# Running count's first copy on ScalarE, the mask on SP's queue, warm-up matmuls behind a pass's scores

## The chip, the core and the metric

The kernel runs on one core of a Trainium2 chip. A core has five engines that run side by side: TensorE (PE; its weight loads are shown apart as PEld), VectorE (DVE), ScalarE (ACT), GpSimd (POOL) and SyncE (SP), which here only issues DMAs. DMAs issued by SP, ACT and POOL go to queues of 16 DMA engines. The metric is the time of one execution in microseconds (us), as the median of several runs.

## The reference, cut to what matters

An attention with two branches feeds a mixture of experts in which each token goes to one expert (top 1).

```python
# q, k, v: 8 batches x 8 heads x 576 positions x 64
q_d = q.reshape(B, H, Sd, 4, D).mean(axis=3)          # k_d, v_d alike
out_d = sm_attn(q_d, k_d, v_d)                        # softmax attention on 144 positions
out_up = np.repeat(out_d, 4, axis=2)
mask = np.abs(pos[:, None] - pos[None, :]) < 4        # local branch: a band of 7 keys
out_local = softmax(where(mask, scale * q @ k.T, -1e9)) @ v
x = (out_up + out_local).transpose(0, 2, 1, 3).reshape(4608, 512)

logits = x @ w_gate                                   # 8 experts
e = argmax(logits); gate = softmax(logits)[e]
y = gate * (relu(x @ w1[e]) @ w2[e])                  # w1[e]: 512x1024, w2[e]: 1024x512
```

## The kernel before

**Attention in passes.** Two heads make one step, so there are 32 steps. They run as a software pipeline written out by hand: the table `PASS` lists pairs `(f, lag)`, and pass i calls `f(i - lag)` for each row of the table in order. That order is the order of the instructions on every engine. Pass i does, among others, in this order: exponentials of the local scores of step i-1 (`exp_loc`, ACT), half the transposes of the pooled branch of step i-3 (`t_d0`, PE), the row maximum of the pooled scores of step i-1 (`max_d`, DVE), the reciprocals `inv` and `inv_d` of step i-2 (DVE), the local scores of step i (`s_loc`, PE: 4 matmuls that put the band's mask into PSUM tile `pS`, line 245, and 20 with the queries and keys, line 251), `pv_loc` and `pv_d` of step i-3 (PE), `norm` (DVE), `max_loc` and `sub_loc` of step i (DVE), `t_loc` of step i-2 (PE), the pooled scores of step i (`s_d`, PE, tile `pD`), `sums` (DVE), `add_up` of step i-3 (DVE, writes `XT`) and the other half of the transposes, `t_d1`. `pS` and `pD` have one buffer each: `s_loc` waits until DVE has read the step before (`sub_loc`), `s_d` until ACT has (`exp_d`).

**Loads.** SP's queue takes, in each pass, queries and keys `qk` of step i+2 (583 KB, 3 buffers), pooled values `vd` of step i+1 (288 KB, 2 buffers; SP waits here for POOL's `vdt`, line 230), a piece of padding or of a weight (`ld_x`), and local values `vw` of step i-1 (320 KB, 2 buffers; SP waits here for `pv_loc`, line 357). POOL adds up the pooled queries, keys and values (`qkt`, `qkd`, `vdt`, `vds`). ACT's queue issues three constants at the start: `cb` (identity and a triangle), `mask` (128x640 of 2 bytes, 160 KB) and `cf` (128x276 of 4 bytes, 138 KB).

**Routing.** Every fourth pass a block of token tiles is ready: gate logits, top expert, and its row in the expert's list. The running count `crun`, 8 numbers in each partition, starts as a copy from the constants `cf` (line 925, after pass 2, on DVE); it is first read some passes later, and POOL adds to it (line 482). POOL then scatters the rows to `xs` (line 550).

**Experts.** After the passes and a tail come, for each of 8 experts, the two layers (lines 674 to 676 and 688 to 690), nearly all of it on PE.

**Warm-up matmuls.** `WARM = (9, 5, 8, 5)`: 9 matmuls of 128x512 on zeros (`wsrc`) before the first pass, then 5, 8 and 5 at the ends of passes 0, 1 and 2. Their results are not used.

```python
    for i in range(NP):
        steps(i)
        if i + 1 < len(WARM):
            warm(WARM[i + 1], i >= 3)
        if i == 2:
            nc.vector.tensor_copy(crun, cf[:, C_CAP:C_CAP + E])
```

Of the kernel before, what the change touches and what calls it, by code (L numbers as in the profile page):

```python
# [11 lines left out]
F32 = mybir.dt.float32  # L12
# [14 lines left out]
NC = NG // 2  # L27
# [15 lines left out]
NEG = -8.0e9  # L43
WARM = (9, 5, 8, 5)

# [45 lines left out]
def attention_moe_kernel(ctx: ExitStack, tc: tile.TileContext, qk, vw, vd, wg, w1, w2, cst, csb, out):  # L91
# [32 lines left out]
    maskb = p1.tile([128, B_END - B_MASK], BF, name="mask", bufs=1)  # L124
    nc.scalar.dma_start(maskb, csb[:, B_MASK:])
    load_qk(1)
# [7 lines left out]

    def warm(n, late=False):
        p = bank() if late else wp
        for _ in range(n):
            nc.tensor.matmul(p, wsrc[:, :128], wsrc, start=True, stop=True)

# [256 lines left out]
    def r_mm(m, tiles):  # L396
        c = tiles[0] * 128
        p = RS[m, "p"] = bank()
        for k, a in [(k, a) for k in (0, 2, 1, 3) for a in range(2)]:
            r = a * 64 + k // 2 * 32  # L400
            nc.tensor.matmul(p[r:r + 32, :256], wgt[:, k, :],
                             XT[m][:, k, c:c + 512].rearrange("p (u a t) -> p a u t", u=2, a=2)[:, a],
                             start=(k % 2 == 0), stop=(k % 2 == 1), tile_position=(0, r), skip_group_check=True)
        for k in range(4) if len(tiles) > 4 else ():
            r = k * 32
            nc.tensor.matmul(p[r:r + 32, 256:384], wgt[:, k, :], XT[m][:, k, c + 512:c + 640],
                             start=True, stop=True, tile_position=(0, r), skip_group_check=True)

    def r_lg(m, tiles):
        lg = RS[m, "lg"] = rp.tile([128, 384], F32, name="over", bufs=1)  # L410
        w = 256 if len(tiles) == 4 else 384
        nc.scalar.activation(lg[:, :w], RS[m, "p"][:, :w], AF.Copy)

    def r_turn(m, tiles):
        lg = RS[m, "lg"]
        p = RS[m, "p"] = bank()
        for u in range(2):
            nc.tensor.matmul(p[:, u * 64:u * 64 + 64], lg[:, u * 128:u * 128 + 128], cf[:, C_PAIR:C_PAIR + 64],
                             start=True, stop=True)
        if len(tiles) > 4:  # L420
            nc.tensor.matmul(p[:, 128:160], lg[:, 256:], cf[:, C_SUM:C_SUM + 32], start=True, stop=True)

    def r_max(m, tiles):
        T = len(tiles)
        RS[m, "pl"] = RS[m, "p"][:, :T * 32].rearrange("p (t e) -> p t e", e=32)[:, :, :E]
        RS[m, "m"] = rp.tile([128, 5], F32, name="rm")
        nc.vector.tensor_reduce(RS[m, "m"][:, :T], RS[m, "pl"], axis=AX.X, op=OP.max)

    def r_sub(m, tiles):
        T = len(tiles)  # L430
        d = RS[m, "d"] = RS[m, "p"][:, 256:296].rearrange("p (t e) -> p t e", e=E)
        nc.vector.tensor_sub(d[:, :T], RS[m, "pl"], RS[m, "m"][:, :T, None].to_broadcast([128, T, E]))

    def r_exp(m, tiles):
        T = len(tiles)
        ex = RS[m, "ex"] = rp.tile([128, 5, E], F32, name="re")
        nc.scalar.activation(ex[:, :T], RS[m, "d"][:, :T], AF.Exp)

    def r_top(m, tiles):
        T = len(tiles)  # L440
        sc = RS[m, "sc"] = RS[m, "p"][:, 320:360].rearrange("p (t e) -> p t e", e=E)
        nc.vector.scalar_tensor_tensor(sc[:, :T], RS[m, "d"][:, :T], 0.0,
                                       cf[:, None, C_DESC:C_DESC + E].to_broadcast([128, T, E]),
                                       op0=OP.is_ge, op1=OP.mult)

    def r_first(m, tiles):
        T = len(tiles)
        nc.vector.tensor_reduce(RS[m, "m"][:, :T], RS[m, "sc"][:, :T], axis=AX.X, op=OP.max)

    def r_hot(m, tiles):  # L450
        T = len(tiles)
        oh = RS[m, "oh"] = rp.tile([128, 5, E], BF, name="oh")
        nc.vector.tensor_tensor(oh[:, :T], RS[m, "sc"][:, :T], RS[m, "m"][:, :T, None].to_broadcast([128, T, E]),
                                op=OP.is_equal)

    def r_gate(m, tiles):
        T = len(tiles)
        gt = RS[m, "gt"] = rp.tile([128, 5], F32, name="gt")
        nc.vector.tensor_reduce(gt[:, :T], RS[m, "ex"][:, :T], axis=AX.X, op=OP.add)

    def r_eps(m, tiles):
        T = len(tiles)
        gt = RS[m, "gt"]
        nc.scalar.activation(gt[:, :T], gt[:, :T], AF.Copy, bias=1e-9)

    def r_place(m, tiles):
        T = len(tiles)
        oh = RS[m, "oh"]
        p = RS[m, "p"] = bank()
        nc.tensor.matmul(p[:, :T * E], trib, oh[:, :T], start=True, stop=False, skip_group_check=True)  # L470
# [30 lines left out]
    def r_last(m, tiles):
# [153 lines left out]

    def split_w2(e, f):
        if (e, f) == (0, 0):
            home("tgi", 2)
            home("ttix", 1)
            home("gap", 16)  # L660
        hi, lo = W2[e, f] = tuple(mp[f // 6].tile([128, DM], F32R, name=f"w2{n}{f}") for n in "hl")
        src = raws[place[2, e, f // 2]][:, (f % 2) * 512:(f % 2) * 512 + 512]
        nc.scalar.activation(hi, src, AF.Copy)  # L663
        nc.vector.tensor_sub(lo, src, hi)  # L664

    def s1(e, f, r=slice(0, FIRST)):
        if e not in HT:
            HT[e] = tuple(mp[0].tile([128, 8, FIRST], F32R, name=f"h{w}") for w in "hl")
        xh, xl = XH[e, 0]
        p = h_bank()[:, :r.stop - r.start]  # L670
        fs = slice(f * 128, (f + 1) * 128)
        for k in range(4):
            wh, wl = W1[e, k]
            nc.tensor.matmul(p, wh[:, fs], xh[:, k, r], start=(k == 0), stop=False)  # L674
            nc.tensor.matmul(p, wh[:, fs], xl[:, k, r], start=False, stop=False)  # L675
            nc.tensor.matmul(p, wl[:, fs], xh[:, k, r], start=False, stop=(k == 3))  # L676
# [216 lines left out]
    def ld_x(i):  # L893
# [180 lines left out]
```

## Time and profile before

| | us |
|---|---|
| median of 3 runs | 649.36 |
| lowest, highest | 646.58, 651.08 |
| profiled execution, its own time | 644.67 |
| span of the core in it, first to last instruction | 642.9 |

The profiled execution is one more run; its span and its own time are 1.8 us apart, which is launch and end. Sums below are made on the trace and so against 644.67. The passes take from 4.7 us to about 175 us of the span, a tail of routing and the first expert's loads to about 245, the experts the rest.

### The profile page before, as it was taken

Reading aid. Unit: us, or ns where it says so; the run is one execution under the profiler, and the core shown is the slowest. Engines: PE = TensorE matmul, PEld = TensorE weight load, DVE = VectorE, ACT = ScalarE, POOL = GpSimd, SP = SyncE. Lnnn points to the kernel's source line nnn. Section 1 sums busy time; section 2 is a strip of 40 time slices with the busy share of each in tenths; the row PEclk is TensorE's granted clock in tenths of the full one; section 3 lists DMA queues with packets and bytes.
Section 4 is the critical chain, followed back from the end, with each engine's and each line's share of the span. In section 5 each row is a group of like instructions: output and inputs, shape, how many; then the busy total and the mean of one; then the engine's idle time right before and its main releaser. Section 6 shows DMA issues by size and latency. Waiting matters only on the chain.

```text
span 642.9 us, 15721 instructions
## 1 busy us (share of the span) xinstructions
PE 617.6 (96%) x6123; PEld 507.9 (79%) x6123; DVE 352.3 (55%) x691; ACT 343.3 (53%) x941; POOL 226.6 (35%) x348
## 2 busy tenths in 40 slices
PE   7899999999979899999999999999999999999994
PEld 4678887787768798888888888888888888888873
DVE  5999988888854573751571174175038166115020
ACT  4899999999964353543452263264235154223120
POOL 7877899999924311111111101101011111110111
PEclk9999999999989999999999999999999999999997
DMA  8998999999862794383274276258137537010001
GB/s 286 286 269 285 292 302 286 292 280 290 239 195 84 187 304 136 122 224 90 84 191 138 66 187 192 68 155 213 56 109 183 181 112 197 35 47 1 34 18 43
DMA packets 68612, 108.65 MB, mean 169 GB/s; under 512 B 15724, under 2 KB 39804, under 8 KB 68496
## 3 DMA queue, kind: packets, MB, share of 16 engines
q1 hardware_dynamic: 62080, 87.78, 49.0%
q0 software_dynamic: 5984, 19.01, 7.9%
q8 instruction: 66, 1.08, 0.8%
q14 instruction: 50, 0.41, 0.2%
q10 hardware_dynamic: 432, 0.37, 0.2%
HBM read 87.09 MB, written 23.67 MB: 172 GB/s over the span
## 4 chain that ended last, share of the span: by engine, by line
PE 68%; issue 10%; POOL 7%; DMA 5%; DVE 5%; ACT 2%; SPq 1%; POOLq 0%; another core or an unknown queue 0%; DVEq 0%; ACTq 0%
PE p L675 8%; PE p L674 8%; PE p L676 8%; PE p L690 7%; PE p L688 7%; PE p L689 7%; POOL xs L550 2%; DMA vd<-in_vd_dram 2%; PE pD L305 2%; POOL vdt L230 2%; PE pX L770 2%; PE pX L789 2%; PE pX L342 1%; PE pS L251 1%; PE pX L329 1%
## 5 line engine op out<-in xcount | busy, mean ns | idle before, releaser
L695 POOL DMA_INDIRECT out_dram<-y,tix x39 | 37.9, 971 | 213.3 <-ACT y L707 201.9
L674 PE MATMUL p<-xh,w1h 128*128 128x512 f32 (+1 forms) x288 | 106.4, 370 | 0.8 <-ACT xh L621 0.7
L675 PE MATMUL p<-xl,w1h 128*128 128x512 f32 (+1 forms) x288 | 105.7, 367 | 0.8 <-DVE xl L622 0.8
L676 PE MATMUL p<-xh,w1l 128*128 128x512 f32 (+1 forms) x288 | 105.5, 366 | 0.0
L688 PE MATMUL p<-w2h,hh 128*128 128x512 f32 x256 | 101.1, 395 | 0.0
L689 PE MATMUL p<-w2l,hh 128*128 128x512 f32 x256 | 99.8, 390 | 0.5 <-DVE w2l L664 0.5
L690 PE MATMUL p<-w2h,hl 128*128 128x512 f32 x256 | 99.9, 390 | 0.0
L679 DVE SCALAR_TENSOR_TENSOR hl<-p,hh 128x512 fp32r<-128x512 f32 (+1 forms) x72 | 45.5, 632 | 94.3 <-ACT hh L678 93.6
L678 ACT ACTIVATE hh<-p 128x512 fp32r<-128x512 f32 (+1 forms) x72 | 39.6, 551 | 78.1 <-PE p L676 75.6
L707 ACT ACTIVATE y<-p,gi 128x512 f32<-128x512 f32 x32 | 22.0, 689 | 91.2 <-PE p L690 86.8
L674 PEld LDWEIGHTS p<-xh,w1h 128*128 128x128 f32 x288 | 54.7, 190 | 10.7 <-ACT xh L621 1.1
L675 PEld LDWEIGHTS p<-xl,w1h 128*128 128x128 f32 x288 | 54.7, 190 | 9.6 <-DVE xl L622 0.9
L676 PEld LDWEIGHTS p<-xh,w1l 128*128 128x128 f32 x288 | 54.6, 190 | 8.7
L689 PEld LDWEIGHTS p<-w2l,hh 128*128 128x128 f32 x256 | 48.1, 188 | 10.6 <-DVE w2l L664 0.9
L690 PEld LDWEIGHTS p<-w2h,hl 128*128 128x128 f32 x256 | 48.1, 188 | 10.2
L688 PEld LDWEIGHTS p<-w2h,hh 128*128 128x128 f32 x256 | 48.1, 188 | 9.5
L664 DVE TENSOR_TENSOR w2l<-raw,w2h 128x512 fp32r<-128x512 f32 x64 | 43.3, 681 | 2.1 <-DMA xs<-xr,ix 1.5
L622 DVE TENSOR_TENSOR xl<-pX,xh 128x512 fp32r<-128x512 f32 x38 | 24.7, 684 | 35.2 <-ACT xh L621 34.2
L194 ACT ACTIVATE w1h<-raw 128x512 fp32r<-128x512 f32 (+1 forms) x72 | 42.1, 584 | 0.0
L550 POOL DMA_INDIRECT xs<-xr,ix x36 | 36.4, 1012 | 15.6 <-ACT xr L525 6.9
L663 ACT ACTIVATE w2h<-raw 128x512 fp32r<-128x512 f32 x64 | 39.8, 626 | 2.8 <-DMA xs<-xr,ix 2.8
L230 POOL TENSOR_TENSOR vdt<-vd 72x512 f32<-72x512 f32 x32 | 40.9, 1279 | 0.3
(152 smaller groups left out, 1240.1 us busy)
## 6 DMA issues: line engine op xcount, KB each, us to landing
raw<-in_w_dram SPq DMA_DIRECT2D x59, 512.0 KB
qk<-in_qk_dram SPq DMA_DIRECT2D x32, 583.0 KB
vw<-in_vw_dram SPq DMA_DIRECT2D x32, 320.0 KB
vd<-in_vd_dram SPq DMA_DIRECT2D x32, 288.0 KB
xrow<-xs SPq DMA_DIRECT2D x32, 192.0 KB
xrow<-xs SPq DMA_DIRECT2D x32, 128.0 KB
xs<-zs SPq DMA_DIRECT2D x6, 512.0 KB
raw<-in_w_dram SPq DMA_DIRECT2D x20, 128.0 KB
```

The lines of the kernel that those rows point to most:

```text
L194: nc.scalar.activation(hi[:, s], src[:, s], AF.Copy)
L230: nc.gpsimd.tensor_add(t2, v[:, 0:2], v[:, 2:4])
L550: ins = nc.gpsimd.indirect_dma_start(out=xs, out_offset=bass.IndirectOffsetOnAxis(ap=IDX[m, t], axis=0), in_=xr, in_offset=None)
L663: nc.scalar.activation(hi, src, AF.Copy)
L664: nc.vector.tensor_sub(lo, src, hi)
L674: nc.tensor.matmul(p, wh[:, fs], xh[:, k, r], start=(k == 0), stop=False)
L675: nc.tensor.matmul(p, wh[:, fs], xl[:, k, r], start=False, stop=False)
L676: nc.tensor.matmul(p, wl[:, fs], xh[:, k, r], start=False, stop=(k == 3))
L679: nc.vector.scalar_tensor_tensor(hl[:, f, r], p, 0.0, hh[:, f, r], op0=OP.max, op1=OP.subtract)
L688: nc.tensor.matmul(p, hh, wh, start=(f == 0), stop=False)
L689: nc.tensor.matmul(p, hh, wl, start=False, stop=False)
L690: nc.tensor.matmul(p, hl, wh, start=False, stop=(f == 7))
```

## The change

It does five things, the last two without effect on any engine's order. `crun` gets its first copy from ACT instead of DVE. The mask is loaded through SP's queue, between the queries of step 0 and those of step 1, instead of ACT's. The warm-up matmuls after pass 0 are 4 instead of 5; those of passes 1 and 2 leave the ends of these passes, and 7 and 5 are issued in passes 2 and 3 by a new step `keep`, right behind `s_loc`. The local values `vw` get a third buffer. Helpers are split into parts that are called in the same order, and the entries of the table `RS` get a longer key.

```diff
-WARM = (9, 5, 8, 5)
+WARM = (9, 4, 7, 5)
...
     maskb = p1.tile([128, B_END - B_MASK], BF, name="mask", bufs=1)
-    nc.scalar.dma_start(maskb, csb[:, B_MASK:])
+    nc.sync.dma_start(maskb, csb[:, B_MASK:])
     load_qk(1)
...
-    def warm(n, late=False):
-        p = bank() if late else wp
+    def warm(n):
         for _ in range(n):
-            nc.tensor.matmul(p, wsrc[:, :128], wsrc, start=True, stop=True)
+            nc.tensor.matmul(wp, wsrc[:, :128], wsrc, start=True, stop=True)
...
-        VW[i] = p2.tile([128, NC, 2, D], F32, name="vw", bufs=2)
+        VW[i] = p2.tile([128, NC, 2, D], F32, name="vw", bufs=3)
...
+    def keep(i):
+        if 2 <= i < len(WARM):
+            warm(WARM[i])
+
     PASS = (
-        (exp_loc, 1), (rb_turn, 5), (t_d0, 3), (rc_place, 6), (eps, 2), (max_d, 1), (inv, 2), (s_loc, 0),
+        (exp_loc, 1), (rb_turn, 5), (t_d0, 3), (rc_place, 6), (eps, 2), (max_d, 1), (inv, 2), (s_loc, 0), (keep, 0),
...
         steps(i)
-        if i + 1 < len(WARM):
-            warm(WARM[i + 1], i >= 3)
+        if i == 0:
+            warm(WARM[1])
         if i == 2:
-            nc.vector.tensor_copy(crun, cf[:, C_CAP:C_CAP + E])
+            nc.scalar.copy(crun, cf[:, C_CAP:C_CAP + E])
```

On DVE, at the turn from pass 2 to pass 3 (`smd<-A` is `sums`, `mxd<-pD` is `max_d`, the reciprocals are `inv` and `inv_d`), before:

```order
L268 TENSOR_TENSOR A<-pS,mx 128x2x5x64
L274 TENSOR_REDUCE smd<-A 128x10
L925 COPY crun<-cf 128x8
L310 TENSOR_REDUCE mxd<-pD 128x3
L282 RECIPROCAL pD<-smd 128x10
L286 RECIPROCAL ivd<-smd 128x3
```

The copy stands between the last step of pass 2 and the first of pass 3. After the change the same place reads:

```order
L267 TENSOR_TENSOR A<-pS,mx 128x2x5x64
L273 TENSOR_REDUCE smd<-A 128x10
L309 TENSOR_REDUCE mxd<-pD 128x3
L281 RECIPROCAL pD<-smd 128x10
L285 RECIPROCAL ivd<-smd 128x3
```

On ACT, at the same place (`AD,smd<-pD,mxd` is `exp_d`, `AT<-pX` is `e_loc`, `A<-A` is `exp_loc`), the copy now stands between the evictions of pass 2 and the exponentials that open pass 3:

```order
L318 ACTIVATE AD,smd<-pD,mxd 128x144 x3
L335 ACTIVATE AT<-pX 128x232
L335 ACTIVATE AT<-pX 128x348
L954 COPY crun<-cf 128x8
L270 ACTIVATE A<-A 128x640
L276 ACTIVATE smd<-smd 128x13
```

On PE, pass 2 and the start of pass 3 before (`pS<-qk` is `s_loc`, `pX<-cf,A` is `t_loc`, `pD<-qkd` is `s_d`, `pX<-cf,AD` are `t_d1` and `t_d0`; the two rows with `wsrc` stand for 5 pairs):

```order
L251 MATMUL pS<-qk 58x64 x20
L329 MATMUL pX<-cf,A 128x128 x5
L305 MATMUL pD<-qkd 64x144 x6
L342 MATMUL pX<-cf,AD 72x112 x3
L138 LDWEIGHTS wsrc
L138 MATMUL pPV<-wsrc 128x512
...
L342 MATMUL pX<-cf,AD 72x112 x3
L245 LDWEIGHTS cb
```

The same stretch after the change and on into pass 3 (the first rows with `wsrc` stand for 7 pairs, the second for 5; `pPV<-AT,vw` is `pv_loc`):

```order
L250 MATMUL pS<-qk 58x64 x20
L137 LDWEIGHTS wsrc
L137 MATMUL pPV<-wsrc 128x512
...
L328 MATMUL pX<-cf,A 128x128 x5
L304 MATMUL pD<-qkd 64x144 x6
L341 MATMUL pX<-cf,AD 72x112 x6
...
L250 MATMUL pS<-qk 58x64 x20
L137 LDWEIGHTS wsrc
...
L356 MATMUL pPV<-AT,vw 64x58 x20
L369 MATMUL pPV<-ADT,vds 64x144 x4
```

The warm-up matmuls have moved from ahead of a pass's scores to behind them: in pass 2 they now stand ahead of `t_loc`, in pass 3 ahead of `pv_loc`, and the 8 that stood ahead of the scores of pass 2 are gone from there. On SP only the mask is new, behind the first `qk`; all later rows keep their order.

## Rows read from the trace of the kernel before

**Rows 1.** Busy time of each engine over the whole span, from the page.

```profile
PE 617.6 (96%) x6123; PEld 507.9 (79%) x6123; DVE 352.3 (55%) x691; ACT 343.3 (53%) x941; POOL 226.6 (35%) x348
```

**Rows 2.** Timeline, 14 to 20 us: start, duration, engine, line, out<-in, [idle before <-releaser].

```profile
14.23 0.82 DVE L264 TENSOR_REDUCE mx<-pS 128x10 f32<-128x640 f32 x1 [0.44 <-PE pS L251]
...
16.53 1.26 POOL L230 TENSOR_TENSOR vdt<-vd 72x512 f32<-72x512 f32 x1
16.56 2.37 DVE L925 COPY crun<-cf 128x8 f32<-128x8 f32 x1
...
17.75 1.14 POOL L219 TENSOR_TENSOR qkt<-qk 128x576 f32<-128x576 f32 x1
...
19.47 0.20 ACT L313 ACTIVATE mxd<-mxd 128x3 f32<-128x3 f32 x1 [2.22 <-DVE mxd L310]
```

**Rows 3.** Chain of work that ended last, in order of time: start, duration, what.

```profile
18.92 0.52 DVE mxd L310
...
23.67 0.53 DVE mxd L310
...
28.42 0.53 DVE mxd L310
...
36.35 0.95 PE pD L305 x12
...
39.59 1.00 PE pX L401 x16
...
41.93 0.91 PE pD L305 x12
...
42.86 0.62 DVE mxd L310
```

**Rows 4.** Timeline of PE, 1 to 23 us.

```profile
1.21 3.56 PE L138 MATMUL pPV<-wsrc 128*128 128x512 bf16 x9 [1.21 <-DVE wsrc L132]
...
7.53 1.25 PE L138 MATMUL pPV<-wsrc 128*128 128x512 bf16 x5
8.71 0.33 PE L245 MATMUL pS<-mask,cb 64*64 64x320 bf16 x4
...
11.44 1.90 PE L138 MATMUL pPV<-wsrc 128*128 128x512 bf16 x8
...
15.23 0.95 PE L305 MATMUL pD<-qkd 64*64 64x144 f32 x12 [0.38 <-issue]
...
16.43 1.24 PE L138 MATMUL pPV<-wsrc 128*128 128x512 bf16 x5
```

**Rows 5.** ACT: copies from `cf`, by tile; then the exponentials that open pass 3.

```profile
L505 ACT COPY xr<-cf x1: 217/217/217, 50.7 to 50.7; 128x4 f32<-128x4 f32 x1
...
15.95 0.74 ACT L271 ACTIVATE A<-A 128x640 f32<-128x640 f32 x1 [0.21 <-DVE A L268]
```

**Rows 6.** Timeline, 4 to 8 us, and the window 5 to 10 (last number GB/s).

```profile
4.70 1.14 POOL L219 TENSOR_TENSOR qkt<-qk 128x576 f32<-128x576 f32 x1 [1.45 <-DMA qk<-in_qk_dram]
5.72 0.33 PE L245 MATMUL pS<-mask,cb 64*64 64x320 bf16 x4 [0.95 <-DMA mask<-in_csb_dram]
...
7.03 1.15 POOL L219 TENSOR_TENSOR qkt<-qk 128x576 f32<-128x576 f32 x1 [0.44 <-DMA qk<-in_qk_dram]
...
5.00:10.00 5.00, 3.85 (x105) 2.58 (x104) 2.49 (x4) 1.57 (x7) 4.29 (x5) 1.00 1.03 325
```

**Rows 7.** SP's waits to 175 us; POOL's timeline at two routed passes; window 72.9 to 175.

```profile
SPq L211 <- PE pPV L357: 25.0, 15, 3.0
...
51.46 0.19 POOL L497 CAST ix<-pos 128x4 int32<-128x4 f32 x1 [2.48 <-DVE pos L492]
...
72.90 0.19 POOL L497 CAST ix<-pos 128x5 int32<-128x5 f32 x1 [1.03 <-DVE pos L492]
...
72.90:175.00 102.10, 98.89 (x2300) 80.99 (x2297) 89.54 (x205) 98.16 (x364) 97.94 (x138) 1.00 0.95 282
```

More of the change, by code (lines that the diff above doesn't have):

```diff
@@ L397, in r_mm @@
         c = tiles[0] * 128
-        p = RS[m, "p"] = bank()
+        p = RS[m, tiles[0], "p"] = bank()
         for k, a in [(k, a) for k in (0, 2, 1, 3) for a in range(2)]:
@@ L409, in r_lg @@
     def r_lg(m, tiles):
-        lg = RS[m, "lg"] = rp.tile([128, 384], F32, name="over", bufs=1)
+        lg = RS[m, tiles[0], "lg"] = rp.tile([128, 384], F32, name="over", bufs=1)
         w = 256 if len(tiles) == 4 else 384
-        nc.scalar.activation(lg[:, :w], RS[m, "p"][:, :w], AF.Copy)
+        nc.scalar.activation(lg[:, :w], RS[m, tiles[0], "p"][:, :w], AF.Copy)
     def r_turn(m, tiles):
-        lg = RS[m, "lg"]
-        p = RS[m, "p"] = bank()
+        lg = RS[m, tiles[0], "lg"]
+        p = RS[m, tiles[0], "p"] = bank()
         for u in range(2):
@@ L424, in r_max @@
         T = len(tiles)
-        RS[m, "pl"] = RS[m, "p"][:, :T * 32].rearrange("p (t e) -> p t e", e=32)[:, :, :E]
-        RS[m, "m"] = rp.tile([128, 5], F32, name="rm")
-        nc.vector.tensor_reduce(RS[m, "m"][:, :T], RS[m, "pl"], axis=AX.X, op=OP.max)
+        RS[m, tiles[0], "pl"] = RS[m, tiles[0], "p"][:, :T * 32].rearrange("p (t e) -> p t e", e=32)[:, :, :E]
+        RS[m, tiles[0], "m"] = rp.tile([128, 5], F32, name="rm")
+        nc.vector.tensor_reduce(RS[m, tiles[0], "m"][:, :T], RS[m, tiles[0], "pl"], axis=AX.X, op=OP.max)
     def r_sub(m, tiles):
         T = len(tiles)
-        d = RS[m, "d"] = RS[m, "p"][:, 256:296].rearrange("p (t e) -> p t e", e=E)
-        nc.vector.tensor_sub(d[:, :T], RS[m, "pl"], RS[m, "m"][:, :T, None].to_broadcast([128, T, E]))
+        d = RS[m, tiles[0], "d"] = RS[m, tiles[0], "p"][:, 256:296].rearrange("p (t e) -> p t e", e=E)
+        nc.vector.tensor_sub(d[:, :T], RS[m, tiles[0], "pl"], RS[m, tiles[0], "m"][:, :T, None].to_broadcast([128, T, E]))
     def r_exp(m, tiles):
         T = len(tiles)
-        ex = RS[m, "ex"] = rp.tile([128, 5, E], F32, name="re")
-        nc.scalar.activation(ex[:, :T], RS[m, "d"][:, :T], AF.Exp)
+        ex = RS[m, tiles[0], "ex"] = rp.tile([128, 5, E], F32, name="re")
+        nc.scalar.activation(ex[:, :T], RS[m, tiles[0], "d"][:, :T], AF.Exp)
     def r_top(m, tiles):
         T = len(tiles)
-        sc = RS[m, "sc"] = RS[m, "p"][:, 320:360].rearrange("p (t e) -> p t e", e=E)
-        nc.vector.scalar_tensor_tensor(sc[:, :T], RS[m, "d"][:, :T], 0.0,
+        sc = RS[m, tiles[0], "sc"] = RS[m, tiles[0], "p"][:, 320:360].rearrange("p (t e) -> p t e", e=E)
+        nc.vector.scalar_tensor_tensor(sc[:, :T], RS[m, tiles[0], "d"][:, :T], 0.0,
                                        cf[:, None, C_DESC:C_DESC + E].to_broadcast([128, T, E]),
@@ L447, in r_first @@
         T = len(tiles)
-        nc.vector.tensor_reduce(RS[m, "m"][:, :T], RS[m, "sc"][:, :T], axis=AX.X, op=OP.max)
+        nc.vector.tensor_reduce(RS[m, tiles[0], "m"][:, :T], RS[m, tiles[0], "sc"][:, :T], axis=AX.X, op=OP.max)
     def r_hot(m, tiles):
         T = len(tiles)
-        oh = RS[m, "oh"] = rp.tile([128, 5, E], BF, name="oh")
-        nc.vector.tensor_tensor(oh[:, :T], RS[m, "sc"][:, :T], RS[m, "m"][:, :T, None].to_broadcast([128, T, E]),
+        oh = RS[m, tiles[0], "oh"] = rp.tile([128, 5, E], BF, name="oh")
+        nc.vector.tensor_tensor(oh[:, :T], RS[m, tiles[0], "sc"][:, :T], RS[m, tiles[0], "m"][:, :T, None].to_broadcast([128, T, E]),
                                 op=OP.is_equal)
@@ L457, in r_gate @@
         T = len(tiles)
-        gt = RS[m, "gt"] = rp.tile([128, 5], F32, name="gt")
-        nc.vector.tensor_reduce(gt[:, :T], RS[m, "ex"][:, :T], axis=AX.X, op=OP.add)
+        gt = RS[m, tiles[0], "gt"] = rp.tile([128, 5], F32, name="gt")
+        nc.vector.tensor_reduce(gt[:, :T], RS[m, tiles[0], "ex"][:, :T], axis=AX.X, op=OP.add)
     def r_eps(m, tiles):
         T = len(tiles)
-        gt = RS[m, "gt"]
+        gt = RS[m, tiles[0], "gt"]
         nc.scalar.activation(gt[:, :T], gt[:, :T], AF.Copy, bias=1e-9)
@@ L467, in r_place @@
         T = len(tiles)
-        oh = RS[m, "oh"]
-        p = RS[m, "p"] = bank()
+        oh = RS[m, tiles[0], "oh"]
+        p = RS[m, tiles[0], "p"] = bank()
         nc.tensor.matmul(p[:, :T * E], trib, oh[:, :T], start=True, stop=False, skip_group_check=True)
@@ L477, in r_cs @@
     def r_cs(m, tiles):
-        cs = RS[m, "cs"] = rp.tile([128, E], F32, name="cs")
-        nc.vector.tensor_reduce(cs, RS[m, "oh"][:, :len(tiles)].rearrange("p t e -> p e t"), axis=AX.X, op=OP.add)
+        cs = RS[m, tiles[0], "cs"] = rp.tile([128, E], F32, name="cs")
+        nc.vector.tensor_reduce(cs, RS[m, tiles[0], "oh"][:, :len(tiles)].rearrange("p t e -> p e t"), axis=AX.X, op=OP.add)
     def r_run(m, tiles):
-        nc.gpsimd.tensor_add(crun, crun, RS[m, "cs"])
+        nc.gpsimd.tensor_add(crun, crun, RS[m, tiles[0], "cs"])
     def r_rk(m, tiles):
         T = len(tiles)
-        rk = RS[m, "rk"] = rp.tile([128, 5, E], F32, name="rk", bufs=1)
-        nc.vector.tensor_mul(rk[:, :T], RS[m, "p"][:, :T * E].rearrange("p (t e) -> p t e", e=E), RS[m, "oh"][:, :T])
+        rk = RS[m, tiles[0], "rk"] = rp.tile([128, 5, E], F32, name="rk", bufs=1)
+        nc.vector.tensor_mul(rk[:, :T], RS[m, tiles[0], "p"][:, :T * E].rearrange("p (t e) -> p t e", e=E), RS[m, tiles[0], "oh"][:, :T])
     def r_pos(m, tiles):
         T = len(tiles)
-        pos = RS[m, "pos"] = rp.tile([128, 5], F32, name="pos")
-        nc.vector.tensor_reduce(pos[:, :T], RS[m, "rk"][:, :T], axis=AX.X, op=OP.add)
+        pos = RS[m, tiles[0], "pos"] = rp.tile([128, 5], F32, name="pos")
+        nc.vector.tensor_reduce(pos[:, :T], RS[m, tiles[0], "rk"][:, :T], axis=AX.X, op=OP.add)
     def r_ix(m, tiles):
@@ L496, in r_ix @@
         ix = rp.tile([128, 5], I32, name="ix")
-        nc.gpsimd.tensor_copy(ix[:, :T], RS[m, "pos"][:, :T])
+        nc.gpsimd.tensor_copy(ix[:, :T], RS[m, tiles[0], "pos"][:, :T])
         for j, t in enumerate(tiles):
@@ L505, in r_last @@
         nc.scalar.copy(xrs[:, sl, DM + 1], cf[:, C_TOK + t0:C_TOK + t0 + T])
-        nc.vector.reciprocal(xrs[:, sl, DM], RS[m, "gt"][:, :T])
+        nc.vector.reciprocal(xrs[:, sl, DM], RS[m, tiles[0], "gt"][:, :T])
     def route_a(m, tiles):
@@ L518, in route_c, with x_tr, x_ev @@
             f(m, tiles)
-    def x_rows(m, t):
-        p = bank()
+    def x_tr(m, t):
+        p = BX["x", m, t] = bank()
         for k in range(4):
             nc.tensor.transpose(p[:, k * 128:(k + 1) * 128], XT[m][:, k, t * 128:(t + 1) * 128], ident)
+    def x_ev(m, t):
+        p = BX.pop(("x", m, t))
         xr = xrs[:, x_slot(m, t)]
@@ L526, in x_rows @@
                              p.rearrange("p (k b d) -> p k b d", k=4, d=32), AF.Copy)
+    def x_rows(m, t):
+        x_tr(m, t)
+        x_ev(m, t)
     prev_sc = []
@@ L656, in split_w2, with w2_open @@
     def split_w2(e, f):
+        w2_open(e, f)
+        w2_part(e, f, 0)
+        w2_part(e, f, 1)
+    def w2_open(e, f):
         if (e, f) == (0, 0):
@@ L660, in split_w2, with w2_part, s1_part @@
             home("gap", 16)
-        hi, lo = W2[e, f] = tuple(mp[f // 6].tile([128, DM], F32R, name=f"w2{n}{f}") for n in "hl")
+        W2[e, f] = tuple(mp[f // 6].tile([128, DM], F32R, name=f"w2{n}{f}") for n in "hl")
+    def w2_part(e, f, n):
+        hi, lo = W2[e, f]
         src = raws[place[2, e, f // 2]][:, (f % 2) * 512:(f % 2) * 512 + 512]
-        nc.scalar.activation(hi, src, AF.Copy)
-        nc.vector.tensor_sub(lo, src, hi)
+        if n == 0:
+            nc.scalar.activation(hi, src, AF.Copy)
+        else:
+            nc.vector.tensor_sub(lo, src, hi)
+    HP = {}
     def s1(e, f, r=slice(0, FIRST)):
+        for n in range(3):
+            s1_part(e, f, r, n)
+    def s1_part(e, f, r, n):
         if e not in HT:
             HT[e] = tuple(mp[0].tile([128, 8, FIRST], F32R, name=f"h{w}") for w in "hl")
[L669 to L676, printed above, removed]
-        hh, hl = HT[e]
-        nc.scalar.activation(hh[:, f, r], p, AF.Relu)
-        nc.vector.scalar_tensor_tensor(hl[:, f, r], p, 0.0, hh[:, f, r], op0=OP.max, op1=OP.subtract)
+        hh, hl = HT[e]
+        if n == 0:
+            xh, xl = XH[e, 0]
+            p = HP[e, f] = h_bank()[:, :r.stop - r.start]
+            fs = slice(f * 128, (f + 1) * 128)
+            for k in range(4):
+                wh, wl = W1[e, k]
+                nc.tensor.matmul(p, wh[:, fs], xh[:, k, r], start=(k == 0), stop=False)
+                nc.tensor.matmul(p, wh[:, fs], xl[:, k, r], start=False, stop=False)
+                nc.tensor.matmul(p, wl[:, fs], xh[:, k, r], start=False, stop=(k == 3))
+        elif n == 1:
+            nc.scalar.activation(hh[:, f, r], HP[e, f], AF.Relu)
+        else:
+            nc.vector.scalar_tensor_tensor(hl[:, f, r], HP.pop((e, f)), 0.0, hh[:, f, r], op0=OP.max, op1=OP.subtract)
     def down(e, hcol, get, between={}):
```

## The prediction

> **What bounds the kernel now.** I read the engines' busy time first. PE is busy for 617.6 of 642.9 us [rows 1]: the experts that follow the passes are PE work without a pause, so whatever the passes save or lose early arrives at the end unless a later wait in the passes swallows it. The change touches only the passes, so the question is what paces them, and that differs by stretch.
>
> The chain of waits says it for the first passes. From 18.92 on it lies on DVE for three turns, and one turn, `max_d` to `max_d`, takes 28.42 - 23.67 = 4.75 us [rows 3]. PE's own turn is little shorter: from `s_d` to the next `s_d` at 36.35 and 41.93 the chain lies on PE alone, 5.58 us, of which 1.00 is a routing product that the early passes do not have: 4.58 us [rows 3]. From a scores product to the `max_d` behind it are 42.86 - 41.93 = 0.93 us. So DVE paces the first passes by 0.17 us per turn, and PE is right behind. From 51 us on POOL has little rest: between 72.9 and 175 us it works 97.94 of 102.10 us while the DMA share is 0.95 [rows 7]. Its visible idle before that is for DVE: 2.48 us at 51.46 and 1.03 us at 72.90, both for `pos`, the last DVE step of a routed block.
>
> **The change, part by part.**
>
> *The copy of `crun`.* Eight numbers in each partition take 2.37 us on DVE, from 16.56 to 18.93 [rows 2]. That is no work: POOL's `vdt` and `qkt` run from 16.53 to 18.89, and the copy ends as they do. ACT then waits 2.22 us for the `max_d` behind the copy. On ACT a copy of this kind took 0.217 us beside a busy POOL, and ACT has a pause of 0.21 us just before 15.95, where the copy now goes [rows 5]: I cost it at nothing there. The other bound is that it waits on ACT as long as on DVE, 2.37 us; nothing in the trace has an ACT copy do that, so I take 0.
>
> With the copy gone, `max_d` of step 2 starts when its scores are there. They start at 15.23 [rows 4] and would let it start at 15.23 + 0.93 = 16.16 instead of 18.92: **2.76 us** earlier. This also takes in the 0.44 us that `max_loc` waited at 14.23 for scores that stood behind 8 warm-ups [rows 2, 4].
>
> *The warm-ups.* After pass 0 one is gone: five took 8.71 - 7.53 = 1.18 us up to the next scores, 0.24 each, and the scores of step 1 start as they end [rows 4]. So everything up to `s_d` of step 2 comes up to 0.24 us earlier; I take 0.2, so 15.03. In pass 2 PE does scores, 7 warm-ups, `t_loc` instead of 8 warm-ups, scores, `t_loc`: with one less in the sum, `t_loc` is not later. In pass 3 it is otherwise. The five warm-ups at 16.43, 1.24 us [rows 4], lay in the hole that the copy made for PE. They are still issued, now behind the scores of step 3, and the hole is gone: they lie in PE's path. PE's next `s_d`, of step 3, is due at 15.03 + 4.58 + 1.24 = 20.85, and `max_d` of step 3 at 20.85 + 0.93 = 21.78. Before, it was at 23.67 [rows 3]. The gain there is **1.89 us**: about one of the three that DVE gets goes back to the warm-ups. From then on DVE's turn of 4.75 is again the longer one, PE gains 0.17 on it per turn, and nothing more is lost. The bounds: 2.76 + 0.2 if the warm-ups find another hole, 1.0 if PE in pass 3 also has to wait for ACT's `exp_d` or for a bank.
>
> *The mask.* The scores of step 0 waited 0.95 us for it, until 5.72; the queries of step 0 were there at 4.70, those of step 1 at 7.03 [rows 6]. On SP's queue it comes behind the first: 160 KB at the 325 GB/s of that window is 0.50 us, so 5.2 at the earliest. Since ACT's queue now brings `cf`, 138 KB, in the mask's old place, 298 KB may have to pass: 0.92 us, 5.6. At worst it lands with the queries of step 1, at 7.0. So its worth lies between +0.5 and -1.3; I take 5.6, the nearest row being its old time, and as the scores of step 1 hang on the warm-ups as well, I add nothing for it.
>
> [...]
>
> *The third buffer for `vw`.* SP waited for `pv_loc` 15 times, 25.0 us [rows 7]. The buffer takes these waits away; SP then stands at the next `vd`, behind POOL's `vdt`, as it does now anyway. A transfer that starts earlier serves nobody unless somebody waited for it, and POOL's waits after 50 us are for `pos`. I cost it at nothing; if POOL's whole idle of 102.10 - 97.94 = 4.16 us were a matter of late loads, it would be worth that. The split helpers and longer keys move no instruction: nothing.
>
> **Sum.** 1.9 us at `max_d` of step 3. At 51.46 POOL waits 2.48 us for DVE, so it takes 1.9 us over whole, and the waits behind it move with it. Profiled execution: 644.67 - 1.9 = 642.8. That execution lies 4.7 us under the median of the three runs (646.58 to 651.08), so I carry the difference: 649.36 - 1.9 = **647.5**.
>
> **The rivals.**
>
> *The passes from 50 us on are paced by POOL and the DMA engines, and take the gain back.* For it: POOL 96% busy, DMA share 0.95. Against: POOL waits for DVE at two places, and 5% of 102 us DMA time, 5 us, is free. Gain 0, from -0.3 to 1.0: 649.4.
>
> *The third buffer is what counts.* If SP's stops starve the DMA engines, the 4.16 us come on top: gain 6.1, 643.3. [...]
>
> *The copy waits on ACT too.* Then `exp_loc` of step 2 moves from 15.95 to about 18.1, and the reciprocals of pass 3 come hardly earlier: gain 0.4, 649.0.
>
> *The mask comes with the queries of step 1.* 1.3 us lost at the front: gain 0.6, 648.8.
>
> [...]
>
> **How the numbers follow.** Forecast (gain 1.0 to 3.0) 0.52; taken back 0.22; third buffer (gain 3 to 6.1) 0.10; copy waits on ACT 0.05; mask late 0.05; clock 0.06. 1% is 6.5 us, about what a measurement of this kernel tells from no change. Faster by that needs the third buffer's full worth and a fast median: 0.04. Slower needs two slow passes or a slow median: 0.04. Same 0.92. The range: gains from -0.5 to 3.5 hold about 8 in 10; the medians of three runs wander by some 2 us of the 4.5 between their extremes, so 643.6 to 651.2.
>
> **What would show it.** `max_d` of step 2 near 16.0 and no DVE copy; the copy on ACT at about 15.8, 0.2 us long; PE without a hole from 15.0 to 20.9, where `s_d` of step 3 starts; `max_d` of step 3 near 21.8; scores of step 0 at 5.2 to 5.6; SP's waits for `pv_loc` gone and those for `vdt` longer; POOL's `ix` near 49.6, after a wait of about 0.6. I am wrong if `ix` comes 1.9 earlier and the end does not, if the copy on ACT takes over 1 us, or if matmuls of passes 1 to 3 take twice their time.

## The result, and the profile after

The changed kernel is slower. Its median is 655.47 us (651.08 to 659.71, 4 runs) where the kernel before gave 647.97 us beside it (645.98 to 651.08, 4 runs): a ratio of 1.0125, 95% interval 1.0078 to 1.0172. The profiled execution took 651.08 us with a span of 649.3, against 644.67 and 642.9 before.

The engines' busy time on the page of the changed kernel, against [rows 1]:

```profile
PE 619.4 (95%) x6118; PEld 508.8 (78%) x6121; DVE 350.2 (54%) x690; ACT 344.2 (53%) x942; POOL 227.2 (35%) x348
```

PE has 1.8 us more busy time and DVE 2.1 us less, about the copy. The rest of the 6.4 us more of span (649.3 against 642.9) is idle time of PE. Timeline of the changed kernel at the places of [rows 2 to 7], all engines:

```profile
5.69 0.33 PE L244 MATMUL pS<-mask,cb 64*64 64x320 bf16 x4 [1.02 <-DMA mask<-in_csb_dram]
...
15.22 0.95 PE L304 MATMUL pD<-qkd 64*64 64x144 f32 x12 [0.63 <-POOL vdt L229]
...
15.60 0.21 ACT L954 COPY crun<-cf 128x8 f32<-128x8 f32 x1
...
16.21 0.61 DVE L309 TENSOR_REDUCE mxd<-pD 128x3 f32<-128x432 f32 x1
...
21.06 0.95 PE L304 MATMUL pD<-qkd 64*64 64x144 f32 x12
...
22.06 0.61 DVE L309 TENSOR_REDUCE mxd<-pD 128x3 f32<-128x432 f32 x1 [0.30 <-PE pD L304]
...
55.22 0.19 POOL L496 CAST ix<-pos 128x4 int32<-128x4 f32 x1 [2.49 <-DVE pos L491]
```

Up to 22 us these rows stand nearly where they were forecast: the copy costs ACT 0.21 us, `max_d` of step 2 comes at 16.21 (18.92 before), `s_d` of step 3 at 21.06, `max_d` of step 3 at 22.06 (23.67 before). But `ix`, due at 49.6, comes at 55.22, later than before. What lies between shows in the chain of work that ended last, from 26 us on (start, duration, what):

```profile
27.30 0.56 PE pS L250 x37
27.86 0.82 issue
28.68 0.32 PE pS L250 x3
...
33.36 0.11 PE pPV L356 x8
33.47 0.86 issue
34.34 0.69 PE pPV L356 x29
...
38.77 0.34 PE pPV L356 x20
39.11 2.15 issue
41.26 0.71 PE pPV L356 x20
41.97 1.86 PE pX L400 x16
```

TensorE stops in the middle of a group of like matmuls, 37 of 40 done and 3 to go, though nothing that the profile shows holds it. Over 20 to 178 us the waits of the changed kernel (engine, line, waited for: us, times, longest) hold, in their second row, a line that the kernel before has only with 0.6 us:

```profile
DVE XT L384 <- ACT outd L373: 9.2, 8, 4.1
...
PE pPV L356 <- issue: 7.6, 6, 2.2
```

Before:

```profile
PE pPV L357 <- issue: 0.6, 2, 0.4
```

The windows between two such stops, and behind the longest, say what they have in common (us, then busy us and number of instructions of PE, PEld, DVE, ACT, POOL; granted clock of PE, DMA share, GB/s):

```profile
34.34:39.11 4.77, 4.77 (x127) 3.84 (x126) 4.33 (x10) 4.16 (x17) 3.27 (x4) 1.00 0.97 280
41.26:47.00 5.74, 5.74 (x66) 3.61 (x67) 1.35 (x4) 2.25 (x6) 2.66 (x4) 0.70 0.92 251
```

From one stop to the next are 126 weight loads, one block of instructions, as it is called from here on. Between the stops before it (27.86 and 33.47) and between three later ones (75.15, 81.77, 88.93) the trace has 126 or 127. The trace has a DMA queue, number 8, that the page calls "instruction": 66 packets of 16 KB in the span, 27 of them between 20 and 178 us, where one comes for some 126 weight loads with their matmuls. This is the DMA view of the changed kernel around one of them, 38.5 to 39.7 us:

```profile
DMA packets 101, 0.31 MB, mean 262 GB/s; under 512 B 15, under 2 KB 15, under 8 KB 100
...
q1 hardware_dynamic: 100, 0.30, 96.8%
q8 instruction: 1, 0.02, 5.7%
```

By the trace's list of packets it started at 38.59 and took 1.09 us, and TensorE went on at 41.26, 1.58 us after it had landed. The packets before it took 1.01 and 1.08 us, and TensorE went on 1.69 and 1.43 us later. So a packet of TensorE's next instructions lands **late**: they start 2.89, 3.15 and 4.25 us after the first weight load of the block before (23.09, 28.68, 34.34), a block lasts some 4.8 us, and 4.25 + 1.09 + 1.58 - 4.77 = 2.15 is the pause of the chain. In this stretch none starts sooner than 0.70 us after its block's first weight load (54.39, block from 53.70). The author's reading is that it is asked for there and stands behind the data, which keep the engines busy for 97% of the window above; no trace shows the asking. An estimate from these times: with 1.1 for the packet and some 1.5 behind it, a delay of over 4.8 - 2.6 = 2.2 us costs time in a block of 4.8 us; the median block between 20 and 178 us lasts 5.4 us in both kernels, and there it may be 2.8.

The traces bear this out beyond these three stops. The stops of all runs below whose warm-ups are not split stand behind the same numbers of weight loads, counted from the start of the span and within one (476, 602, 728 and so on), whatever the program does there. And in these 15 traces TensorE enters none of 393 blocks between 20 and 178 us sooner than 0.99 us after the block's packet has landed.

The second row of the windows shows what stands behind this long pause: the granted clock is 0.70 in these 5.74 us, and 0.50 in 42.00 to 44.00. `r_mm` took 1.86 us in the chain, against 1.00 before [rows 3], and DVE then waited 4.1 us.

Counted alike in both traces (pauses of over 0.6 us between two weight loads, between 20 and 178 us, at the end of a block, that end 0.8 to 2.0 us after a packet has landed): before 1 of 1.2 us, after 6 of 9.0 us. The last `s_d` starts at 176.40 before and at 183.81 after. The 7.4 us are about these 7.8 more, with some slow clock, less the 1.5 us won at 25 us (`s_d` of step 4 at 25.39, 26.86 before).

### The profile page after: what moved, and what is told of

It is laid out like the page before. It is cut to its first block, busy times and chain, and to the rows that moved or that the text cites. A ratio compares the mean times of both kernels' runs of the same rounds, so it can differ in the third digit from the quotient of the medians.

```text
span 649.3 us, 15741 instructions
## 1 busy us (share of the span) xinstructions
PE 619.4 (95%) x6118; PEld 508.8 (78%) x6121; DVE 350.2 (54%) x690; ACT 344.2 (53%) x942; POOL 227.2 (35%) x348
## 3 DMA queue, kind: packets, MB, share of 16 engines
q8 instruction: 66, 1.08, 0.7%
HBM read 87.09 MB, written 23.67 MB: 171 GB/s over the span
## 4 chain that ended last, share of the span: by engine, by line
PE 73%; issue 9%; ACT 7%; DMA 4%; DVE 3%; POOL 2%; SPq 0%; POOLq 0%; another core or an unknown queue 0%; DVEq 0%; ACTq 0%
PE p L699 8%; PE p L698 8%; PE p L700 8%; PE p L715 7%; PE p L713 7%; PE p L714 7%; PE pD L304 3%; PE pX L328 2%; PE pPV L369 2%; ACT AD L318 2%; PE pX L341 2%; PE pPV L356 2%; PE pX L795 2%; PE pX L814 2%; PE pS L250 2%
## 5 line engine op out<-in xcount | busy, mean ns | idle before, releaser
L678 ACT ACTIVATE w2h<-raw 128x512 fp32r<-128x512 f32 x64 | 39.7, 624 | 2.7 <-DMA xs<-xr,ix 2.7
```

## The experiments

Runs named a_ are the changed kernel with an edit, those named b_ the kernel before with one; those with cw in the name, and a_vw2_mask_act, have of the change only the copy and the warm-ups. In the table "late" is that count and its us, "delay" the mean time from a block's first weight load to the start of its packet, both for one profiled execution between 20 and 178 us; "before" is the kernel before on the same chip. No trace of b_split2 is used.

| run | median us | before | ratio (95% interval) | late | delay us |
|---|---|---|---|---|---|
| before | | | | 1, 1.2 | 2.33 |
| after | 655.47 | 647.97 | 1.0125 (1.0078 to 1.0172) | 6, 9.0 | 2.61 |
| a_again | 654.36 | 645.22 | 1.0152 (1.0116 to 1.0189) | 5, 7.7 | 2.47 |
| a_vw2 | 651.14 | 645.81 | 1.0083 (1.0052 to 1.0115) | 6, 10.6 | 2.60 |
| b_vw3 | 650.86 | 645.81 | 1.0069 (1.0041 to 1.0097) | 8, 10.8 | 2.71 |
| b_crun | 645.57 | 645.81 | 1.0004 (0.9982 to 1.0025) | 2, 3.1 | 2.55 |
| b_warm | 646.15 | 645.81 | 1.0001 (0.9970 to 1.0032) | 4, 6.3 | 2.42 |
| b_mask | 647.31 | 646.24 | 1.0021 (0.9988 to 1.0055) | 3, 3.2 | 2.45 |
| a_vw2_mask_act | 649.74 | 646.24 | 1.0073 (1.0042 to 1.0104) | 5, 5.3 | 2.31 |
| b_qk4 | 647.19 | 646.24 | 0.9991 (0.9957 to 1.0025) | 6, 5.6 | 2.54 |
| a_vw_lag2 | 661.97 | 646.24 | 1.0276 (1.0201 to 1.0351) | 4, 4.9 | 2.76 |
| a_cw_late | 648.67 | 646.20 | 1.0039 (1.0004 to 1.0074) | 4, 4.1 | 2.24 |
| a_noraw | 653.07 | 646.20 | 1.0103 (1.0020 to 1.0186) | 3, 5.9 | 2.45 |
| b_noraw | 644.64 | 646.20 | 0.9965 (0.9928 to 1.0002) | 2, 1.9 | 2.37 |
| b_heavy | 653.22 | 646.20 | 1.0118 (1.0081 to 1.0155) | 8, 10.5 | 2.86 |
| a_split2 | 652.08 | 645.22 | 1.0078 (1.0043 to 1.0113) | 5, 3.7 | 2.63 |
| a_split4 | 662.97 | 645.22 | 1.0279 (1.0248 to 1.0310) | 11, 13.3 | 3.09 |
| cw_split4 | 663.14 | 645.22 | 1.0288 (1.0247 to 1.0330) | 10, 13.8 | 3.06 |
| b_split2 | 650.24 | 649.10 | 1.0017 (0.9978 to 1.0056) | | |
| cw_split2 | 653.34 | 649.10 | 1.0052 (1.0012 to 1.0093) | 3, 5.6 | 2.69 |

The trace is one execution and the median another matter: that of a_vw2_mask_act took 644.80 us, the fastest of its runs. Trace by trace the two go together: over the 18 of the table other than a_vw_lag2 the start of the last `s_d`, 176.40 to 190.58 us, follows the late us with a correlation of 0.91. The mean delay says less, since a few blocks make the late us.

**The parts one by one.** First the third buffer, taken from the changed kernel and given to the kernel before:

```diff
-        VW[i] = p2.tile([128, NC, 2, D], F32, name="vw", bufs=3)
+        VW[i] = p2.tile([128, NC, 2, D], F32, name="vw", bufs=2)
```

> The changed kernel with two vw buffers again, all else as changed. Theory A (the third buffer lets the vw loads start earlier, TensorE's instruction packets on the DMA engines land later, and TensorE stands idle at the ends of its instruction blocks): the idle stretches of TensorE marked issue between 20 and 178 us go from some 12.7 us back to about 4, the clock stays at 1.00 in 40 to 45 us, and the time is 645.5 to 647.5 us, 0.5 to 2.5 under the kernel before. Theory B (TensorE, 1.1 to 1.5 us ahead after the copy and the warm-ups have moved, outruns its instruction packets whatever the buffers are): the idle stretches stay, 652 to 658 us.

> The kernel before with three vw buffers and nothing else of the change. Theory A: TensorE's idle stretches marked issue appear at the ends of its instruction blocks, the time is 652 to 659 us. Theory B (being ahead is what hurts): the time stays within 2 us of the kernel before, no new idle stretches. If half of each: 650 to 652 us.

Both theories fell as they stood. The buffer alone costs 5.0 us by the medians, with A's stops at the ends of blocks, though less than A's 652 to 659 us: it lies in the range for half of each. Without the buffer the changed kernel stays 5.3 us above the kernel before, between the two ranges. SP's waits in 20 to 178 us show what the buffer does, in b_vw3:

```profile
SPq L207 <- POOL vdt L230: 72.9, 25, 5.0
SPq L119 <- PE pS L251: 22.4, 12, 5.6
```

The wait for `pv_loc` [rows 7] is gone, and SP is held instead at the load of `qk`, until `s_loc` has read its buffer: one load of `vw`, 320 KB, is on its way more than before.

The copy, the warm-ups and the mask, each alone on the kernel before:

```diff
-            nc.vector.tensor_copy(crun, cf[:, C_CAP:C_CAP + E])
+            nc.scalar.copy(crun, cf[:, C_CAP:C_CAP + E])
```

> The kernel before with the first copy of the running count on ScalarE and nothing else of the change. Theory A: s_d of step 3 starts 0.5 to 1 us earlier than 22.11 us, no new idle stretches of TensorE, 646.5 to 648 us. Theory B: TensorE is ahead, idle stretches marked issue appear, 650 us or more.

> The kernel before with the warm-up matmuls moved and counted as in the change, and nothing else of it. Theory A: no new idle stretches, within 1.5 us of the kernel before. Theory C (the places of the warm-ups shift what lies in an instruction block, and with it where TensorE waits): idle stretches marked issue appear, 650 us or more.

> The kernel before with the mask loaded on SP's queue between the first two qk loads and nothing else of the change. [...] Theory A2 (the mask, 160 KB ahead of qk of pass 1 on the one queue, shifts how the loads and the packets meet from the first pass on): 648 to 652 us, idle stretches of TensorE marked issue at the ends of blocks. Theory D (the mask is hidden; what is left in the changed kernel without the third buffer comes from the copy and the warm-ups together): within 1.5 us of the kernel before.

Neither the copy nor the warm-ups alone change the time, against the 650 us of B and C, though in their traces `s_d` of step 3 starts at 20.69 and 21.10 instead of 22.11, the first more than had been expected. (This start scatters: in traces of b_vw3, b_qk4, b_mask and b_heavy, which have neither part, it lies at 22.81, 22.22, 21.22 and 21.10; in after, a_again and a_vw2_mask_act, which have both, at 21.06, 20.88 and 20.91, but in a_vw2 and a_vw_lag2, which have both too, at 23.56 and 22.36.) The chain in b_crun shows where such a lead goes:

```profile
32.52 0.56 PE pS L251 x34
33.08 0.11 PE pPV L357 x6
33.19 1.94 issue
35.12 0.90 PE pPV L357 x16
```

The mask's 1.1 us can't be told from nothing; they fit D, though the interval reaches to 3.6 us. Then the copy and the warm-ups together: the changed kernel with two `vw` buffers and the mask back on ScalarE's queue.

> The changed kernel with two vw buffers and the mask on ScalarE's queue: of the change only the copy and the warm-ups are left. Theory A2: within 2 us of the kernel before, 644 to 647.5 us. Theory D: 649 to 653 us, as the changed kernel with two vw buffers (651.1 us).

D held: the pair costs 3.5 us by the medians (ratio 1.0073), though each of its halves costs nothing that can be told. Its own trace can't show how, being a fast one; in that of a_vw2, which has the pair and the mask and took 654.80 us, the late packets are 6 of 10.6 us. With the buffer's 0.69% that is 1.42%, and the mask's 0.21% at most adds to it; the change measured 1.25 and 1.52%.

**Is it loads on their way, or the buffer?** One more buffer for `qk` in the kernel before (`bufs=3` to `bufs=4`), and the changed kernel with each `vw` load a pass later:

```diff
-        (pool_qk2, -1), (rc_ix, 6), (t_loc0, 2), (e_loc1, 2), (e_loc0, 2), (ld_vw, 1), (sub_loc, 0),
+        (pool_qk2, -1), (rc_ix, 6), (t_loc0, 2), (e_loc1, 2), (e_loc0, 2), (ld_vw, 2), (sub_loc, 0),
```

> The kernel before with four qk buffers in place of three and nothing of the change. Theory A (more loads outstanding delay the instruction packets, whichever buffer lets them go): the packets start 0.3 to 1 us later after the block's first instruction than before (mean of 20 to 178 us), 648 to 653 us. Rival: only a third vw buffer moves SP, since SP is held by the wait for the vw buffer; then no load goes earlier and the time is within 1.5 us of the kernel before.

> The changed kernel, three vw buffers, but each vw load issued one pass later in SP's order (the pass before it is used), so that its data is not outstanding for longer. Theory A: the packets' delay falls back to that of before, fewer idle stretches, 645 to 649 us on this chip, where the changed kernel as it is would give 651 to 653. Rival (what hurts is not how many loads are outstanding): 651 us or more. If vw lands too late for pv_loc, TensorE waits for the DMA there, 655 us or more.

The rival held for b_qk4: SP is held at `vw`, as before (24.4 us for `pv_loc` against 25.0), and the time stays. In a_vw_lag2 `vw` comes too late, as had been allowed for; the wait answers to none in the kernel before:

```profile
PE pPV L356 <- DMA vw<-in_vw_dram: 8.7, 9, 2.3
```

That run says nothing on the packets.

**Less and more data.** Five loads of expert weights left out in passes 11 to 30 (zeros in place of these weights, so that the output is another; the routing and the passes are the same), and 320 KB more in every second pass:

```diff
     def raw_part(k, j):
+        if j == 0 and k > 0:
+            raws.append(raws[0])
+        return
...
     nc.vector.memset(onesb, 1.0)
+    raws.append(wpool.tile([128, 1024], F32, name="raw", bufs=5))
+    nc.vector.memset(raws[0], 0.0)
```

```diff
         nc.sync.dma_start(VD[i].rearrange("p r c h d -> p (r c h d)"), vd[i])
+        if i % 2 == 1:
+            idle = p1.tile([128, NC, 2, D], F32, name="idle", bufs=1)
+            nc.sync.dma_start(idle.rearrange("p c h d -> p (c h d)"), vw[i])
```

> The changed kernel without the first five loads of expert weights (128 KB a pass in passes 11 to 30, about a tenth of what the DMA engines move there; these weights are zeros instead, and one tile is cleared on VectorE at the start). If the data on the DMA engines delays the instruction packets: from 73 us on the packets start 0.3 to 1 us sooner after their block's first instruction than in the changed kernel, the late ones at 75 to 90 us are fewer or gone, and the time falls by 2 to 4 us against the changed kernel. Rival (the packets' lateness has nothing to do with the amount of data): the delays and the time stay.

> The kernel before, without the same five loads. If only late packets cost time there: 0 to 2 us faster than before, since before has few late packets from 73 us on. If the passes are bound by the DMA engines' rate: a tenth less data gives up to 20 x 0.3 us, 4 to 6 us faster.

> The kernel before with 320 KB more loaded in every second pass (160 KB a pass, an eighth more; nobody reads it). Theory A: instruction packets start later (mean delay from 2.5 to over 3 us), more of them late, 652 to 662 us. If the DMA engines have room for it and delay nothing: within 2 us of the kernel before.

The window 73 to 95 us, where the first of these loads run, in the changed kernel:

```profile
73.00:95.00 22.00, 17.66 (x393) 14.24 (x390) 15.45 (x34) 17.79 (x62) 17.43 (x25) 1.00 0.97 296
```

and in a_noraw:

```profile
73.00:95.00 22.00, 21.87 (x555) 18.09 (x544) 20.02 (x49) 21.47 (x82) 18.07 (x24) 1.00 0.84 251
```

With 15% less moved, TensorE does 544 weight loads in 22 us instead of 390. The delay of the packets there is 3.8 us in the changed kernel, 4.0 in a_again, 3.8 in b_vw3, 2.1 in the kernel before and 1.3 in a_noraw; late ones are 3, 3, 3, 0 and 0. The three with the third buffer and all the data stop at the same three ends of blocks, behind 1486, 1613 and 1739 weight loads; of the eight unsplit traces with two `vw` buffers and the usual data none stops for over 0.6 us at more than two of them, and seven at one or none, the kernel before at none. But it is not the rate of the DMA engines that makes the difference. The same window of the kernel before:

```profile
73.00:95.00 22.00, 21.89 (x514) 18.18 (x511) 19.28 (x45) 21.36 (x80) 20.85 (x29) 1.00 0.98 293
```

It moves as much, 293 GB/s against 296 and 290 in a_again, at a share of 0.98, without a late packet; and b_vw3 differs from it in the third buffer alone. So less data takes the late packets away here, and the buffer brings them without more data per us. The whole time does not give such a proof: a_noraw's 3.2 us against a_again (by the ratios) lie within the intervals; its trace had other late packets ahead of 73 us (one pause of 3.4 us at 27.5). b_noraw speaks against the DMA rate as such: 1.6 us instead of 4 to 6. b_heavy came out as theory A said in time, 7.0 us slower, and in late packets, 8 of 10.5 us; the mean delay rose from 2.33 to 2.86 us, not to over 3. But it is mixed: POOL's waits for `qk` also grew, from 6.5 us to 15.7.

**The lead.** Five warm-ups more in a_vw2_mask_act (`WARM = (9, 4, 7, 10)`):

> Of the change only the copy and the warm-ups (two vw buffers, the mask on ScalarE's queue), and five more warm-up matmuls behind the scores of pass 3, which hold TensorE back by about 1.1 us, that is, by what the two parts had won it. Theory B (the lead over the loads is what makes the instruction packets land late): back to within 1.5 us of the kernel before, 645 to 648 us. Theory E (any shift of the instructions in the blocks or of the loads deals the late packets anew; the lead as such does nothing): stays near the 649.7 us of the same kernel without the five, 648 to 652 us.

It took the lead back (`s_d` of step 3 at 21.96, 22.11 before). Its 648.67 us lie within E's range, 0.7 above B's, and the interval, 0.3 to 4.8 us above the kernel before, reaches into both. That decides nothing; but b_crun and b_warm, which have the lead and lose nothing, speak against B.

**The place of the block's end.** The same warm-up columns in more matmuls, which shifts the end of each block within its pass:

```diff
         for _ in range(n):
-            nc.tensor.matmul(wp, wsrc[:, :128], wsrc, start=True, stop=True)
+            for c in range(4):
+                nc.tensor.matmul(wp[:, c * 128:c * 128 + 128], wsrc[:, :128], wsrc[:, c * 128:c * 128 + 128],
+                                 start=True, stop=True)
```

> The changed kernel once more, beside the kernel before on this chip: 652 to 656 us where before gives 646.5; four or more late packets between 20 and 178 us, though not all in the same passes.

> The changed kernel with each warm-up matmul of 512 columns made two of 256: the same columns, 25 more weight loads ahead of pass 4, so that TensorE crosses into a new instruction block 25 weight loads earlier in each pass. Theory F (the point of the pass at which the packet is asked for decides): the time moves by over 3 us from the changed kernel's, either way, with the mean delay of the packets. Theory G (the amount of data outstanding decides, all points alike): within 2 us of the changed kernel.

> As a_split2, four of 128 columns: 75 more weight loads, the block's end 75 earlier in each pass, more than half a block. Theory F: the time moves by over 3 us from the changed kernel's, and differs from a_split2's. Theory G: within 2 us of the changed kernel.

> Of the change only the copy and the warm-ups (two vw buffers, the mask on ScalarE's queue; 649.7 us where before gave 646.2), each warm-up of 512 columns made four of 128. Theory F: moves by over 2 us; if the packets then mostly land in time, TensorE's lead of 1.5 us at 25 us remains to the end, 643 to 646 us, faster than the kernel before. Theory G: 648.5 to 651 us.

> The kernel before with each warm-up matmul of 512 columns made two of 256 (27 more weight loads ahead of the passes, the same columns), nothing of the change. Theory F (the point of the pass at which a packet is asked for decides how late it lands, and the kernel before has a good one): 648 to 653 us, three or more late packets. Theory G (the amount of data alone): within 1.5 us of the kernel before.

> Of the change the copy and the warm-ups alone, each warm-up made two of 256 columns. Theory F: the time moves from the 649.7 us of the unsplit pair (ratio 1.0073 to before) by 1.5 us or more; if by luck most packets land in time, 643.5 to 645 us, since the lead of 1.5 us then stays. Theory G: ratio 1.005 to 1.010.

The large shift does much: 8.6 us on the changed kernel, some 14 on the pair. Some 2.4 us of that lie at the front (`s_d` of step 4 at 27.61 in cw_split4 and at 25.24 without the split), the rest behind it, with 11 and 10 late packets. The stop is no longer at `pv_loc`; the chain of a_split4 has it between `pv_d` and `t_loc`:

```profile
109.58 0.68 PE pPV L371 x8
110.26 2.39 issue
112.66 0.71 PE pX L330 x5
```

The small shift took 2.3 us off the changed kernel by the medians and 4.8 by the ratios (1.0152 and 1.0078, intervals apart), the only gain of the kind, so that F's 3 is missed by one count and met by the other; on the kernel before and on the pair it did nothing that can be told, as G says. So F holds for the large shift, and for the small one it stays open. No version beat both kernels; what lies lowest with all its work, b_crun, is the kernel before in time.

## Why the prediction was wrong

*What bounds the kernel.* That what the passes win or lose reaches the end held, in the wrong direction: from the last `s_d` to the end are 466.5 us before and 465.5 after. Not seen: TensorE also stops until packets of its own instructions have landed, 6 times for 9.0 us in the changed kernel. In the kernel before the mean delay was 2.33 us, where by the estimate above a block of 4.8 us leaves room for 2.2 and the median block for 2.8: DMA share 0.95 [rows 7] was read as 5% free and not as data that may stand in front of something.

*The third buffer, "a transfer that starts earlier serves nobody ... I cost it at nothing".* This is the step that failed, and it failed below the bound given for it: its ends were 0 and a gain of 4.16 us, it cost 5.0 (b_vw3; ratio 1.0069). A transfer that starts earlier serves nobody, and these runs speak for it standing in front of somebody. Shown: the cost of the buffer alone (b_vw3), the held load (SP's waits), the late packets at the same places in three traces with it, and their going there when data is taken away (a_noraw). Argued: that the packet waits behind the load that is on its way more; no trace follows the two through a DMA engine.

*The copy.* Right in mechanism and nearly in size: 2.71 us earlier at `max_d` of step 2, where 2.76 was forecast, 0.21 us on ACT. *The warm-ups.* Right: 1.61 us at `max_d` of step 3, where 1.89 was forecast. SP's waits went as said: 0.3 us for `pv_loc` in the changed kernel, and 77.8 us for `vdt` instead of 71.5. *The sum.* The step "nothing more is lost" from there to POOL's `ix` is the second that failed: alone, each part's lead is worth nothing at the end, together they cost 3.5 us. Why the pair does what its halves don't is open; the late packets of its one trace, 5 of 5.3 us, belong to an execution without the loss, and those of a_vw2, 6 of 10.6 us, say how time was lost there, not why.

*The mask.* It landed at 5.69 where 5.6 was forecast and 5.72 was before; its 1.1 us at the end can't be told from nothing. It came 0.03 us earlier, so that of the bounds, a gain of 0.5 and a loss of 1.3 us, neither was seen.

*The rivals.* "Taken back" was near what the copy and the warm-ups did alone, though in the chain of b_crun a late packet took it, not POOL's pace. "The third buffer counts" had the right part with the wrong sign. The chance of 0.06 for the clock and the two slow passes that "slower" counts on were the author's estimate, and no run shows such a pass: in both kernels the granted clock reads 1.00 from 5 to 41 us, passes 1 to 3 among them. It was lower later, 0.70 in 41.26 to 47.00 of the changed kernel, behind a pause of 2.15 us. The range ended at 651.2 since no case had a stall of TensorE that is not a wait on another engine.

## What to carry to other kernels

Where the DMA engines are as busy as here (share 0.95 in [rows 7]), a deeper buffer may not be free, and here it cost 5.0 us: before adding one, look at what else uses them, the engines' own instructions included, and ask what the load that now starts sooner will stand in front of. An idle stretch named "issue" in the middle of like instructions, which comes again after the same number of weight loads (126 or 127), was here a late instruction packet; compare its place with the "instruction" packets before looking for a wait. In such a stage a lead won at the front may be spent at the next late packet, so time an edit alone and with its companions.

## What the runs showed of the hardware that was not expected

A packet of TensorE's instructions, 16 KB for some 126 weight loads and their matmuls, took 0.9 to 1.4 us and started, between 20 and 178 us of the changed kernel, 0.70 to 4.43 us after the first weight load of the block before; TensorE entered no block sooner than 0.99 us after its packet had landed (15 traces, 393 blocks). The packet of a block thus came while the block before it ran; that did not hide it in the passes of the changed kernel, with up to 2.15 us in the chain and 9.0 us in sum.

The delays of these packets at 73 to 95 us are 3.8 us in the changed kernel (296 GB/s), 2.1 in the kernel before (293 GB/s, one `vw` load less on its way) and 1.3 in a_noraw (251 GB/s). So the delay seems to go with the data that is on its way, not with the rate alone; by what mechanism no run shows.

After a pause of 2.15 us TensorE's granted clock was 0.70 over the next 5.74 us, with 0.50 in 42.00 to 44.00, and `r_mm` took 1.86 us instead of 1.00. After the pauses of 0.82 and 0.86 us ahead of it the granted clock was 1.00 (28.68 to 33.47 and 34.34 to 39.11), and after one of 1.86 us at 81.90 too (83.76 to 86.00). So a pause did not always bring the lower clock, and in the kernel before, between 20 and 175 us, the granted clock is 1.00.
